# Agent attention with a squared-ReLU FFN: background blocks taken in pairs, four single banks a set, and a reordered start

## The chip, the cores and the metric

The kernel runs on one core of a Trainium2 chip. The metric is the device time of one execution in microseconds (us); a comparison uses the median of several runs. Engines are named as in the profile: PE (matmul), PEld (its weight loads), DVE (vector), ACT (scalar), POOL (GpSimd), SP (issues DMAs). [...]

## What is computed

```python
def _attn_ref(q, k, v, agents):                # B, N, C = 4, 12480, 128; 49 agents
    scale = 1.0 / np.sqrt(q.shape[-1])
    def sm(a, b):
        s = scale * (a @ b.transpose(0, 2, 1))
        s = s - s.max(-1, keepdims=True)
        e = np.exp(s)
        return e / (e.sum(-1, keepdims=True) + 1e-09)
    a2k = sm(agents, k)
    agent_v = a2k @ v
    q2a = sm(q, agents)
    return (q2a @ agent_v).astype(np.float32)

def _moe_ref(x, w_in, w_out):                  # 49920 tokens, d_ff 2048
    h = np.maximum(x @ w_in, 0.0)
    return (h * h @ w_out).astype(np.float32)
```

## The kernel before, in words

The agents' values of a batch (49 x 128) are multiplied with `w_in` into tables (`aw_hi`, and `aw_ex` for the rest of their precision). The first product of the FFN is then table times query weights: `w` (128 rows) against `aw_hi`, and the strips `x` (19 rows) against `aw_ex`. Each fp32 product of the second half is made of three rounded ones: `g_lo` x `wo_hi`, `g_hi` x `wo_lo`, `g_hi` x `wo_hi`.

**Sessions.** The main loop (lines 766 to 827) runs 211 sessions of up to 8 chunks of 128 hidden units for 480 tokens; 52 of them make a batch. The first four (EARLY) have 4 chunks, sessions 4 to 207 have 8. In session s, PE makes the `first` product (line 393) into bank set x and then y, four banks each; the sets A and B alternate. Then PE makes the `second` product (line 433) of session s-2: 24 matmuls of 480 columns (12 if that session had 4 chunks), all into bank 0 of x, after ACT has rectified it. ACT rectifies the banks (`rectified`, line 417, one instruction per entry of GROUPS, line 161) and squares the result `r` (line 421). DVE rounds `r` of the session before into `g_hi`, subtracts twice for `g_lo` (lines 808 to 823, "low part" below), and at the end of the session copies or adds bank 0 into `ob` (line 447), which frees that bank for the set that takes it next. So a bank 0 that DVE frees late holds up the `first` product of the next session, whose second set is that bank's.

**Attention beside it.** Everything else is cut into steps with a session and a phase ("P" on PE, "D" on DVE, "A1", "A3" on ACT, "L" for loads). After LEAD = 6 matmuls of `second`, phase "P" runs. There stand, for short:
- Q: query scores of a group of 960 tokens, 64 records of matmuls with 49 columns in the trace (32 in the order, since each is recorded twice), once in four sessions. DVE then makes `m`, `e`, ACT the exponential, DVE `z` (four instructions) and `pp`;
- T: one of two transpositions of `pp` per group; ACT casts the bank to `w`;
- K and V: a block of 1024 keys (scores, ACT copy `s`, DVE running maximum `mx`) or of values (DVE difference `d`, ACT exponential, matmuls, DVE `av` and `mx`) of the next batch, 13 each, also 64 records of 49 columns;
- W: one of four tables of the next batch.

`plan` (lines 729 to 739) gives the queries their sessions: scores AHEAD = 6 sessions ahead of use. `allowed` (line 741) lets the background of the next batch take one step in each even session, and in an odd one if it is behind its schedule; BEGIN and SPARE shift this schedule. So Q, K and V come in sessions of their own or together, one block each.

**The start.** `head` (lines 533 to 706) makes the agents' values of batch 0 with banks of its own, decodes the weights, which come as pairs of 32-bit words, in chunks of 512 columns (ACT, four or five DVE instructions, then `kept`: a cast on ACT and two instructions on POOL), and makes tables 0 and 1 and `aw_ex`. Tables 2 and 3 are made in sessions 0 and 1 in a spare set B. While s < 4 the sessions use set A alone, B takes those tables, the first query scores and the outputs `o` of sessions 2 and 3 (two banks, by turns). The tiles of the last weight chunk, called `s` in the trace, come from pool `sp`, which is closed with the head; the pool of `r` and `g_lo` is opened after that in the same memory.

Of the kernel before, what the change touches and what calls it, by code (L numbers as in the profile page):

```python
# [9 lines left out]
F32 = mybir.dt.float32  # L10
# [7 lines left out]
P = 128  # L18
TP = 120
NT = 8  # L20
# [8 lines left out]
AHEAD = 6  # L29
# [7 lines left out]
BEGIN = 4  # L37
SPARE = 3
# [3 lines left out]
def agent_attention_relu2(ctx: ExitStack, tc: tile.TileContext, qT, kT, v, agT, w_in, w_out, outT):  # L42
# [49 lines left out]
    ps_h = head.enter_context(tc.tile_pool(name="ps_h", bufs=3, space=PSUM))  # L92
    ps_o = head.enter_context(tc.tile_pool(name="ps_o", bufs=1, space=PSUM))
    ps_a = head.enter_context(tc.tile_pool(name="ps_a", bufs=1, space=PSUM))
# [53 lines left out]
    def kept(at, t, rest):  # L148
# [6 lines left out]
        act.copy(hi, t)  # L155
        pool.tensor_sub(t, t, hi.bitcast(F32))
        pool.tensor_add(lo, t, rest)
# [3 lines left out]
    GROUPS = ((0, 1), (1, 1), (2, 2))  # L161
# [9 lines left out]
    def bank():  # L171
        if alone[0]:
            return ps_h.tile([P, 2, 512], F32, name="h")[:, 0, :]
        return desk["at"][BLOCKS]
# [31 lines left out]
    def scores(b, i, kt):  # L206
        st = state.setdefault(b, {"s": []})
        _, rows, nt = blocks[i]
        sv = bank()[:rows, : nt * NA].rearrange("p (t a) -> p t a", a=NA)
        for t in range(nt):  # L210
            tiled(sv[:, t, :], kt[:, t * rows : (t + 1) * rows], ag[:, b, :])
        s = sp.tile([P, NT * NA], F32, name="s").rearrange("p (t a) -> p t a", a=NA)
        st["s"].append(s)
        if i == 0:
            st["mx"] = small.tile([P, NT, NA], F32, name="mx")
        s, mx = (x[:rows, :nt, :] for x in (s, st["mx"]))
        yield "A1", 0
        act.copy(s, sv)
        yield "D", 0
        if i == 0:  # L220
            dve.tensor_copy(mx, s)
        else:
            dve.tensor_max(mx, mx, s)

    def maxima(b):
        st = state[b]
        m1 = small.tile([P, NA], F32, name="m1")
        dve.reduce_max(m1, st["mx"].rearrange("p t a -> p a t"), axis=AX.X)
        yield "P", 1, True
# [7 lines left out]
        yield "P", 1, True  # L237
# [19 lines left out]
    def whole_sums(b):  # L257
# [7 lines left out]
        yield "P", 1, True  # L265
# [7 lines left out]
    def values(b, i, vt):  # L273
        st = state[b]
        _, rows, nt = blocks[i]
        yield "D", 0, True
        es = st["mx"][:rows, :nt, :]
        e = small.tile([P, NT, NA], F32, name="d", bufs=2)[:rows, :nt, :] if i else es
        less_maximum(b, i, e, spare())
        yield "A3", 0  # L280
        act.activation(e, e, AF.Exp, scale=scale)
        yield "P", 1
        pv = bank()
        for t in range(nt):
            tiled(pv[:C, :NA], vt[:rows, t, :], e[:, t, :], start=(t == 0), stop=(t == nt - 1))
        yield "D", 0
        if i == 0:
            st["av"] = small.tile([C, NA], F32, name="av")
            dve.tensor_copy(st["av"], pv[:C, :NA])
        else:  # L290
            dve.tensor_add(st["av"], st["av"], pv[:C, :NA])
            spare().tensor_add(es, es, e)

    def tables(b):
# [4 lines left out]
        for n in range(FF // 512):  # L299
            yield "P", 1, True  # L300
# [19 lines left out]
    def queries(g):  # L320
# [24 lines left out]
        for j in range(2):  # L345
            yield
            pt = query_bank(TURNED)
# [110 lines left out]
    def background(b):  # L458
        kt = load_keys(b, 0, kv, "kt")
        for i in range(NK):  # L460
            yield "P", 1, True
            nxt = load_keys(b, i + 1, kv, "kt") if i + 1 < NK else load_values(b, 0, kv, "vt")
            yield from scores(b, i, kt)
            kt = nxt
        yield from maxima(b)
        vt = kt
        for i in range(NK):
            nxt = load_values(b, i + 1, kv, "vt") if i + 1 < NK else None
            yield from values(b, i, vt)
            vt = nxt  # L470
        yield from whole_sums(b)
        yield from tables(b)

    EVENTS = 2 * NK + 3 + FF // 512
# [18 lines left out]
    even = const.tile([P, 512], F32R, name="even")  # L493
    nc.gpsimd.memset(even.bitcast(F32), 1.0)

# [5 lines left out]
    idled(ps_a, (512,) * 7 + (G,) * 4)  # L501

# [4 lines left out]
    def table(n, pieces=1):  # L507
        near = aw.tile([P, 512], F32R, name="aw_lo", bufs=3)
        pws = [bank() for _ in range(pieces)] if n < 2 else [desk["at"][4 - n]]
        w = 512 // pieces  # L510
# [10 lines left out]
    def rest_of_tables():  # L521
        near = aw.tile([P, 512], F32R, name="aw_lo", bufs=3)
        pw = ps_a.tile([P, 512], F32, name="psa")
# [9 lines left out]
    with tc.tile_pool(name="pre", bufs=PRE) as pre, tc.tile_pool(name="dec", bufs=2) as dec:  # L533
        H = P // 2
# [34 lines left out]
        def keeps(at):  # L569
            kept(at, *raws.pop(at))  # L570
# [15 lines left out]
        todo["next"] = (*next(todo["gen"]), 0)  # L586
# [106 lines left out]
        bounds(2 * FF - WIDE)  # L693
# [17 lines left out]
    sets = ctx.enter_context(tc.tile_pool(name="sets", bufs=1, space=PSUM))  # L711
# [17 lines left out]
    for g in range(1, B * NB):  # L729
        gen = queries(g) if g > 1 else ahead  # L730
        u = starts[g] - AHEAD
        if g > 1:
            plans(gen, (u - 2, "L"))
        t0, t1 = u + 3, u + 5
        if g == 1:
            u, t0, t1 = 1, 4, 5
        plans(gen, (u, "P"), (u, "D"), (u, "A3"), (u + 1, "D"), (u + 1, "A3"), (u + 2, "D"))
        for t in (t0, t1):
            plans(gen, (t, "P"), (t, "A1"), (t, "A1"))

    def allowed(s):
        if s < todo["start"]:
            return False
        if s % 2 == 0:
            return True
        return todo["done"] < (s - todo["start"] + 1) * EVENTS / (todo["end"] - todo["start"] - SPARE)

    def phase(name, s):
        for gen in plan.pop((s, name), ()):
            step(gen)  # L750
        while todo["next"]:
            (at, lead, *event), since = todo["next"][:-1], todo["next"][-1]
            if at != name or s < since + lead:
                break
            if event:
                if not allowed(s if name == "P" else s + 1):
                    break
                todo["done"] += 1
            said = step(todo["gen"])
            todo["next"] = said and (*said, s)  # L760

    made, x, early = {}, None, None
    todo["end"] = starts[NB]
    for s in range(len(sessions) + LAG):
# [3 lines left out]
        if s in starts and s // 2 and starts.index(s) % NB == 0:  # L768
            assert not todo["next"]
            b = starts.index(s) // NB  # L770
            if b + 1 < B:
                todo.update(gen=background(b + 1), done=0, start=s, end=starts[(b + 1) * NB])
                todo["next"] = (*step(todo["gen"]), s)
        phase("L", s)

        tags = "AB" if s <= len(EARLY) or (s - len(EARLY)) % 2 == 0 else "BA"
        x = Banks(tags[0])
        other = lambda: Banks(tags[1])
        if s == 0:
            early = other()  # L780
        desk["at"] = early if s < len(EARLY) else x
        o = desk["at"][s % LAG if s < len(EARLY) else 0][:, :G]
# [6 lines left out]
        if s < LAG:  # L789
            alone[0] = True  # L790
            if s:
                for _ in range(5):
                    pe.matmul(desk["at"][0][:, :P], ones, ones, start=True, stop=True)
            table(s + 2)
            alone[0] = False
# [7 lines left out]
        if m == 2:  # L803
            squared(r, 0, 2 * SET)
        elif m:
            for n in (0, 2):
                squared(r, n, 2)
        if 1 <= s <= len(sessions):
            z, n = sessions[s - 1]
            old = made.pop(s - 1)  # L810
            hi = held("g_hi", F32R, n, place(z)[2] % (2 * SET))
            los = [ffn.tile([P, SET, G], F32R, name="g_lo", bufs=3) for _ in range(n)]
            parts[z] = hi, los
            if n == 2:
                rounded(hi, old, 0, 2 * SET)
                rest(los[0], old, hi, 0, SET)
                phase("D", s)
                rest(los[1], old, hi, SET, SET)
            else:
                for i in (0, 2):  # L820
                    rounded(hi, old, i, 2)
                    rest(los[0], old, hi, i, 2)
                phase("D", s)
# [3 lines left out]
        phase("A3", s)  # L827

# [34 lines left out]
```

## Time and profile before

| | us |
|---|---|
| median of 3 runs (1887.86 to 1888.83) | 1888.68 |
| the profiled execution's own time | 1887.94 |
| its span | 1885.8 |
| PE busy | 1859.1 |
| DVE busy | 1715.7 |
| ACT busy | 1623.9 |
| POOL busy | 21.0 |

The profiled execution is 0.74 us below the median, and 2.1 us of its time lie outside the span. A timeline row gives start, length and instruction, rows of one kind in a row merged with their count; neighbouring instructions of an engine overlap at their ends, so the cost of one is read from start to start. A bracket names idle time ahead of the instruction and the engine that ended it.

### The profile page before, as it was taken

The numbers are of one execution on the slowest core, as the hardware profiler recorded it, in microseconds if no ns is written. First come the engines' busy times: TensorE is split into PE (matmuls) and PEld (weight loads), VectorE is DVE, ScalarE is ACT, GpSimd is POOL, SyncE is SP. The second block draws the span as 40 slices with busy tenths as digits, with TensorE's granted clock in tenths as the row PEclk, the third lists the DMA queues.
The fourth block names the chain that finished last, engine by engine and source line by source line (L and its number), as shares of the span: only waits on it lengthen the run. The fifth ranks groups of instructions, "written<-read, shape, count | busy, mean of one in ns | idle before, by whom it ended". The sixth has DMA issues, their size and how long they took to land.

```text
span 1885.8 us, 39996 instructions
## 1 busy us (share of the span) xinstructions
PE 1859.1 (99%) x17186; PEld 1464.5 (78%) x17186; DVE 1715.7 (91%) x1487; ACT 1623.9 (86%) x1834; POOL 21.0 (1%) x24
## 2 busy tenths in 40 slices
PE   8899999999999999999999999999999999999998
PEld 4577877877778878777778787878777877877787
DVE  7799899999899899999998899999999999999997
ACT  5688888888888888888898888888888998999996
POOL 2100000000000000000000000000000000000000
PEclk9999999999999999999999999999999999999999
DMA  9222212211122222321112221322111111111100
GB/s 374 87 90 85 82 54 77 94 61 52 54 72 78 87 61 67 95 70 59 56 42 78 94 64 33 94 73 68 52 40 43 46 39 51 40 44 45 37 27 24
DMA packets 54820, 131.47 MB, mean 70 GB/s; under 512 B 6508, under 2 KB 34828, under 8 KB 54644
## 3 DMA queue, kind: packets, MB, share of 16 engines
q1 hardware_dynamic: 54644, 128.93, 21.4%
q8 instruction: 135, 2.21, 0.5%
q14 instruction: 41, 0.34, 0.1%
HBM read 80.97 MB, written 25.56 MB: 56 GB/s over the span
## 4 chain that ended last, share of the span: by engine, by line
PE 90%; DVE 8%; ACT 1%; issue 1%; POOL 0%; DVEq 0%; ACTq 0%; POOLq 0%
PE A L63 46%; PE B L63 42%; DVE g_lo L63 3%; DVE g_hi L63 2%; DVE ob L63 1%; DVE mx L63 1%; DVE z L63 1%; DVE e L63 1%; DVE t L63 0%; PE h L63 0%; ACT r L63 0%; DVE rest L63 0%; PE o L63 0%; PE psa L63 0%; DVE d L63 0%
## 5 line engine op out<-in xcount | busy, mean ns | idle before, releaser
L63 DVE TENSOR_TENSOR g_lo<-r,g_hi 128x1920 fp32r<-128x1920 f32 (+1 forms) x422 | 894.5, 2126 | 7.5
L63 ACT ACTIVATE r<-r 128x3840 f32<-128x3840 f32 (+1 forms) x217 | 719.5, 3319 | 2.2
L63 ACT ACTIVATE r<-B 128x480 f32<-128x480 f32 (+1 forms) x618 | 393.3, 723 | 132.1 <-PE B L63 132.1
L63 ACT ACTIVATE r<-A 128x480 f32<-128x480 f32 (+1 forms) x630 | 400.8, 723 | 71.4 <-PE A L63 71.4
L63 DVE CAST g_hi<-r 128x3840 fp32r<-128x3840 f32 (+1 forms) x217 | 448.6, 2067 | 1.7 <-ACT r L63 1.7
L63 PE MATMUL A<-g_hi,wo_lo 128*128 128x480 f32 x832 | 328.4, 395 | 0.0
L63 PE MATMUL B<-g_hi,wo_lo 128*128 128x480 f32 x832 | 324.9, 390 | 1.3 <-ACT r L63 0.7
L63 PE MATMUL A<-g_hi,wo_hi 128*128 128x480 f32 x832 | 317.2, 381 | 0.0
L63 PE MATMUL B<-g_hi,wo_hi 128*128 128x480 f32 x832 | 316.6, 381 | 0.0
L63 PE MATMUL A<-w,aw_hi 128*128 128x480 f32 x840 | 230.0, 395 | 3.6 <-ACT r L63 2.0
L63 PE MATMUL B<-w,aw_hi 128*128 128x480 f32 x824 | 223.8, 393 | 0.0
L63 PE MATMUL A<-g_lo,wo_hi 128*128 128x480 f32 x832 | 215.1, 380 | 0.6 <-ACT r L63 0.6
L63 PE MATMUL B<-g_lo,wo_hi 128*128 128x480 f32 x832 | 214.9, 380 | 0.6 <-ACT r L63 0.6
L63 PEld LDWEIGHTS A<-w,aw_hi 128*128 128x128 f32 x840 | 150.0, 188 | 59.5 <-issue 34.0
L63 PEld LDWEIGHTS B<-w,aw_hi 128*128 128x128 f32 x824 | 146.7, 188 | 49.8 <-issue 30.7
L63 PEld LDWEIGHTS A<-g_hi,wo_lo 128*128 128x128 f32 x832 | 156.6, 188 | 30.2 <-issue 2.4
L63 PEld LDWEIGHTS B<-g_hi,wo_lo 128*128 128x128 f32 x832 | 156.5, 188 | 27.4 <-DVE g_hi L63 1.3
L63 PEld LDWEIGHTS A<-g_hi,wo_hi 128*128 128x128 f32 x832 | 156.6, 188 | 25.6 <-issue 2.2
L63 PEld LDWEIGHTS A<-g_lo,wo_hi 128*128 128x128 f32 x832 | 156.2, 188 | 25.9 <-ACT r L63 0.9
L63 PEld LDWEIGHTS B<-g_lo,wo_hi 128*128 128x128 f32 x832 | 156.2, 188 | 25.8 <-ACT r L63 0.9
L63 PEld LDWEIGHTS B<-g_hi,wo_hi 128*128 128x128 f32 x832 | 156.3, 188 | 23.4 <-issue 0.7
L63 DVE COPY ob<-A 128x480 f32<-128x480 f32 x103 | 67.7, 657 | 61.6 <-PE A L63 58.3
(169 smaller groups left out, 1280.6 us busy)
## 6 DMA issues: line engine op xcount, KB each, us to landing
qt<-in_qT SPq DMA_DIRECT2D x52, 480.0 KB
out_T<-ob SPq DMA_DIRECT2D x104, 240.0 KB
kt<-in_kT SPq DMA_DIRECT2D x36, 512.0 KB
vt<-in_v SPq DMA_DIRECT2D x36, 512.0 KB
x<-w SPq DMA_DIRECT2D x416, 35.6 KB
ahead<-in_kT SPq DMA_DIRECT2D x12, 512.0 KB
ahead<-in_v SPq DMA_DIRECT2D x12, 512.0 KB
w<-w SPq DMA_DIRECT2D x104, 56.2 KB
```

Source lines behind the costliest of these rows:

```text
L63: ins = issue(*args, **kw)
```

## The change

1. Background blocks: `room(s)` gives two blocks to the sessions that have query scores, and one to an even session if the schedule is behind; no block stands in another session. `scores` and `values` take a group of one or two, the second in the bank TURNED. The loads are issued by `more()` in phase "L".
2. GROUPS has four single banks, so a set is rectified by four instructions instead of three.
3. Queries: AHEAD is 8, the transpositions stand one session apart, the second in bank ASKED; FIRSTS gives the first three groups their sessions. BEGIN is 6, SPARE 9.
4. Head: its banks are closed before the tables, which go into set B (table 0 in banks 0 and 1, `aw_ex` in 2, table 1 in 0, tables 2 and 3 in banks 2 and 3). The last weight chunk is bounded, decoded and kept behind the tables, and kept by DVE alone.
5. Start: a session with 4 chunks makes its low part itself, not the session after; sessions 0 and 1 square ahead of their table; sessions 4 and 5 square and round in halves and end with eight small matmuls on `ones`.

```diff
-AHEAD = 6
+AHEAD = 8
-BEGIN = 4
-SPARE = 3
+BEGIN = 6
+SPARE = 9
...
-    GROUPS = ((0, 1), (1, 1), (2, 2))
+    GROUPS = ((0, 1), (1, 1), (2, 1), (3, 1))
...
-    def scores(b, i, kt):
...
+    def scores(b, group):
+        st = state.setdefault(b, {"s": []})
+        outs = []
+        for (i, kt), slot in zip(group, (BLOCKS, TURNED)):
+            _, rows, nt = blocks[i]
+            sv = bank(slot)[:rows, : nt * NA].rearrange("p (t a) -> p t a", a=NA)
+            for t in range(nt):
+                tiled(sv[:, t, :], kt[:, t * rows : (t + 1) * rows], ag[:, b, :])
+            outs.append(sv)
...
-            pt = query_bank(TURNED)
+            pt = query_bank((TURNED, ASKED)[j])
...
-        bounds(2 * FF - WIDE)
         warm(ps_a, 3)
         pa = bank()
         pe.matmul(pa[:, :P], avs, spread, start=True, stop=True)
         warm(ps_a, 2)
         turn["avT"] = small.tile([C, P], F32, name="av0")
         dve.tensor_copy(turn["avT"], pa[:, :P])
+        banks.close()
+        sets = ctx.enter_context(tc.tile_pool(name="sets", bufs=1, space=PSUM))
+        early = desk["at"] = Banks("B")
+        table(0, (0, 1))
+        rest_of_tables()
+        table(1, (0,))
+        bounds(2 * FF - WIDE)
         makes(2 * FF - WIDE)
-
-        table(0, 2)
-        rest_of_tables()
-        keeps(2 * FF - WIDE)
-        table(1)
+        keeps(2 * FF - WIDE, dve)
...
+    def room(s):
         if s < todo["start"]:
-            return False
-        if s % 2 == 0:
-            return True
...
+            return 0
+        if s % 4 == starts[1] % 4:
+            return 2
+        late = todo["done"] < (s - todo["start"] + 1) * 2 * NK / (todo["end"] - todo["start"] - SPARE)
+        return int(late and s % 2 == 0)
...
+    def idle(n):
+        for _ in range(n):
+            pe.matmul(desk["at"][BLOCKS][:, :P], ones, ones, start=True, stop=True)
+
+    def low_parts(z, s=None):
...
         if s < LAG:
+            if s:
+                idle(5)
+                phase("P", s)
+            for n in (0, 2):
+                squared(r, n, 2)
             alone[0] = True
...
-            table(s + 2)
+            table(s + 2, (s + 2,))
...
+        if s - 1 in made:
+            low_parts(s - 1, s)
+        if m == 1:
+            low_parts(s)
         run(work)
         if s >= LAG:
             copied_out(*sessions[s - LAG], o)
         phase("A3", s)
+        if len(EARLY) <= s < BEGIN:
+            idle(8)
```

**The end of the head on DVE.** `s` is the last weight chunk, `aw_hi` and `aw_ex` are tables. Before:

```order
L63 SCALAR_TENSOR_TENSOR s<-vt,s 128x512
L63 TENSOR_SCALAR s<-s 128x512
L63 SCALAR_TENSOR_TENSOR s<-vt,s 128x512
L63 SCALAR_TENSOR_TENSOR aw_hi<-h,signs,aw_lo 128x256 x2
L63 TENSOR_TENSOR aw_ex<-psa,aw_lo 128x512
L63 SCALAR_TENSOR_TENSOR aw_hi<-h,signs,aw_lo 128x512
L63 SCALAR_TENSOR_TENSOR aw_hi<-B_741,signs,aw_lo 128x512
```

Now:

```order
L68 SCALAR_TENSOR_TENSOR aw_hi<-B_686,signs,aw_lo 128x512
L68 TENSOR_SCALAR s<-s 128x512 x2
L68 SCALAR_TENSOR_TENSOR s<-vt,s 128x512
L68 TENSOR_SCALAR s<-s 128x512
L68 SCALAR_TENSOR_TENSOR s<-vt,s 128x512
L68 CAST wo_hi<-s 128x512
L68 TENSOR_TENSOR s<-s,wo_hi 128x512
L68 TENSOR_TENSOR wo_lo<-s 128x512
L68 SCALAR_TENSOR_TENSOR aw_hi<-B_688,signs,aw_lo 128x512
```

The decode stood ahead of the tables and now stands behind table 1, and the three instructions that keep the chunk follow it on DVE. The first rectification on ACT (`r_750<-A0`), which takes memory of these tiles, has among the engines it waits for DVE and POOL before, and the same now.

**Sessions 2 and 3 on DVE**, from the `z` of the first group to the second output. Before:

```order
L63 TENSOR_TENSOR e<-e,z 120x392
L63 COPY ob<-B_739 128x480
L63 CAST g_hi<-r 128x960
L63 TENSOR_TENSOR g_lo<-r,g_hi 128x960
L63 CAST g_hi<-r 128x960
L63 TENSOR_TENSOR g_lo<-r,g_hi 128x960
L63 TENSOR_TENSOR pp<-e,pp 120x8x49
L63 TENSOR_TENSOR ob<-B_740,ob 128x480
```

Now:

```order
L68 TENSOR_TENSOR e<-e,z 120x392
L68 CAST g_hi<-r 128x960
L68 TENSOR_TENSOR g_lo<-r,g_hi 128x960
L68 CAST g_hi<-r 128x960
L68 TENSOR_TENSOR g_lo<-r,g_hi 128x960
L68 COPY ob<-B_686 128x480
L68 TENSOR_TENSOR pp<-e,pp 120x8x49
L68 CAST g_hi<-r 128x960
L68 TENSOR_TENSOR g_lo<-r,g_hi 128x960
L68 CAST g_hi<-r 128x960
L68 TENSOR_TENSOR g_lo<-r,g_hi 128x960
L68 TENSOR_TENSOR ob<-B_687,ob 128x480
```

One whole low part, four instructions, that of session 3, now stands ahead of the second `ob`.

**A block in the value phase, on PE** (T and V in one session). Before:

```order
L63 MATMUL B_8243<-identr,pp 98x120 x4
L63 MATMUL B_8242<-d,vt 32x49 x32
L63 MATMUL B_8241<-g_hi,wo_lo 128x480
L63 MATMUL B_8241<-g_hi,wo_hi 128x480
L63 MATMUL B_8241<-g_hi,wo_lo 128x480
```

Now, in a session with query scores:

```order
L68 MATMUL A_3635<-ag,qt 24x49
L68 MATMUL A_3634<-d,vt 32x49 x32
L68 MATMUL A_3636<-d,vt 32x49 x32
L68 MATMUL A_3633<-g_hi,wo_lo 128x480
L68 MATMUL A_3633<-g_hi,wo_hi 128x480
```

Two blocks follow the scores directly, each in its own bank. **On DVE the session ahead of such a pair** now holds the group's `pp` and two `d`:

```order
L68 CAST g_hi<-r 128x3840
L68 TENSOR_TENSOR g_lo<-r,g_hi 128x1920
L68 TENSOR_TENSOR pp<-e,pp 120x8x49
L68 TENSOR_TENSOR d<-s,mb 128x392 x2
L68 TENSOR_TENSOR g_lo<-r,g_hi 128x1920
L68 TENSOR_TENSOR ob<-B_4464,ob 128x480
```

Before, the fullest session of a cycle in that phase held the group's `z` and one block:

```order
L63 CAST g_hi<-r 128x3840
L63 TENSOR_TENSOR g_lo<-r,g_hi 128x1920
L63 TENSOR_REDUCE z<-e 120x8
L63 TENSOR_SCALAR z<-z 120x8
L63 RECIPROCAL z<-z 120x8
L63 TENSOR_TENSOR e<-e,z 120x392
L63 TENSOR_TENSOR av<-av,B_3932 128x49
L63 TENSOR_TENSOR mx<-mx,d 128x392
L63 TENSOR_TENSOR d<-s,mb 128x392
L63 TENSOR_TENSOR g_lo<-r,g_hi 128x1920
L63 TENSOR_TENSOR ob<-B_3931,ob 128x480
```

The `d` of a pair moved into a session that has no Q, K, V or T on PE.

## Rows read from the trace of the kernel before

**Rows 1.** PE timeline, starts of sessions 52 to 55 (start, us, instruction)

```profile
509.15 1.03 PE L63 MATMUL A<-w,aw_hi 128*128 128x480 f32 x4
...
517.98 1.02 PE L63 MATMUL B<-w,aw_hi 128*128 128x480 f32 x4
...
526.15 1.03 PE L63 MATMUL A<-w,aw_hi 128*128 128x480 f32 x4
...
533.97 1.03 PE L63 MATMUL B<-w,aw_hi 128*128 128x480 f32 x4
```

**Rows 2.** PE timeline, Q and K together in session 8

```profile
124.00 0.90 PE L63 MATMUL A<-ag,qt 128*32 128x49 f32 x64
124.71 0.87 PE L63 MATMUL A<-ag,kt 128*32 128x49 f32 x64
```

**Rows 3.** DVE timeline, sessions 6 and 7

```profile
108.29 0.56 DVE L63 TENSOR_TENSOR pp<-e,pp 120x392 fp32r<-120x392 f32 x1
108.77 0.56 DVE L63 TENSOR_TENSOR mx<-mx,s 128x392 f32<-128x392 f32 x1
...
112.03 0.66 DVE L63 COPY ob<-A 128x480 f32<-128x480 f32 x1 [0.63 <-PE A L63]
...
114.79 4.23 DVE L63 TENSOR_TENSOR g_lo<-r,g_hi 128x1920 fp32r<-128x1920 f32 x2
```

**Rows 4.** PE timeline, session 38, with one V, and the start of 39

```profile
385.74 1.03 PE L63 MATMUL A<-w,aw_hi 128*128 128x480 f32 x4
...
387.35 0.49 PE L63 MATMUL B<-x,aw_ex 19*128 19x480 f32 x4 [0.17 <-DVE ob L63]
...
395.03 1.03 PE L63 MATMUL B<-w,aw_hi 128*128 128x480 f32 x4
```

**Rows 5.** Groups by form, ACT, 105 to 1860 us (busy us, mean ns | idle before, releaser)

```profile
L63 ACT ACTIVATE r<-B 128x480 f32<-128x480 f32 x406 | 212.1, 584 | 131.2 <-PE B L63 131.2
...
L63 ACT ACTIVATE r<-B 128x960 f32<-128x960 f32 x203 | 203.3, 1001 | 0.0
```

**Rows 6.** DVE timeline, head: an earlier chunk's decode, and table 1

```profile
33.95 0.88 DVE L63 TENSOR_SCALAR t<-t 128x512 f32<-128x512 f32 x2
...
36.05 0.69 DVE L63 SCALAR_TENSOR_TENSOR rest<-raw,rest 128x512 f32<-128x512 uint32 x1
...
60.06 0.75 DVE L63 SCALAR_TENSOR_TENSOR aw_hi<-h,signs,aw_lo 128x512 fp32r<-128x512 f32 x1 [0.44 <-ACT aw_lo L63]
```

**Rows 7.** ACT timeline, first rectifications of sessions 0 and 1

```profile
62.55 1.89 ACT L63 ACTIVATE r<-A 128x480 f32<-128x480 f32 x3 [2.52 <-PE A L63]
...
66.90 1.88 ACT L63 ACTIVATE r<-A 128x480 f32<-128x480 f32 x3
```

**Rows 8.** DVE timeline, sessions 2 and 3

```profile
78.18 0.55 DVE L63 TENSOR_REDUCE z<-e 120x8 f32<-120x392 f32 x1
...
79.69 0.65 DVE L63 COPY ob<-B 128x480 f32<-128x480 f32 x1
...
84.26 0.65 DVE L63 TENSOR_TENSOR ob<-B,ob 128x480 f32<-128x480 f32 x1
```

**Rows 9.** PE timeline, sessions 1 and 4 to 8

```profile
66.28 1.38 PE L63 MATMUL B<-ones 128*128 128x128 f32 x10
...
84.96 0.48 PE L63 MATMUL B<-x,aw_ex 19*128 19x480 f32 x3 [1.46 <-DVE ob L63]
...
86.55 0.60 PE L63 MATMUL A<-g_hi,wo_lo 128*128 128x480 f32 x1
...
92.56 1.03 PE L63 MATMUL B<-w,aw_hi 128*128 128x480 f32 x4
...
100.11 1.03 PE L63 MATMUL A<-w,aw_hi 128*128 128x480 f32 x4
...
104.17 0.49 PE L63 MATMUL B<-x,aw_ex 19*128 19x480 f32 x4 [1.80 <-DVE ob L63]
...
120.03 1.03 PE L63 MATMUL A<-w,aw_hi 128*128 128x480 f32 x4
```

More of the change, by code (lines that the diff above doesn't have):

```diff
@@ L146, in decoded, with kept @@
         return t.bitcast(F32), rest
-    def kept(at, t, rest):
+    def kept(at, t, rest, *only):
         n = t.shape[1]
@@ L271, in whole_sums, with values @@
         dve.reciprocal(rl, rl)
-    def values(b, i, vt):
+    def values(b, group):
         st = state[b]
[L275 to L279, printed above, removed]
-        yield "A3", 0
[L281 to L285, printed above, removed]
-        yield "D", 0
[L287 to L292, printed above, removed]
+        es, outs = [], []
+        for i, _ in group:
+            _, rows, nt = blocks[i]
+            e = small.tile([P, NT, NA], F32, name="d", bufs=2) if i else st["mx"]
+            es.append(e[:rows, :nt, :])
+            less_maximum(b, i, es[-1], spare())
+        yield "A3", 0
+        for e in es:
+            act.activation(e, e, AF.Exp, scale=scale)
+        yield "P", 1, "told"
+        for (i, vt), e, slot in zip(group, es, (BLOCKS, TURNED)):
+            _, rows, nt = blocks[i]
+            pv = bank(slot)
+            for t in range(nt):
+                tiled(pv[:C, :NA], vt[:rows, t, :], e[:, t, :], start=(t == 0), stop=(t == nt - 1))
+            outs.append(pv)
+        yield "D", 0
+        for (i, _), pv in zip(group, outs):
+            if i == 0:
+                st["av"] = small.tile([C, NA], F32, name="av")
+                dve.tensor_copy(st["av"], pv[:C, :NA])
+            else:
+                dve.tensor_add(st["av"], st["av"], pv[:C, :NA])
+        for (i, _), e in zip(group, es):
+            if i:
+                _, rows, nt = blocks[i]
+                all_e = st["mx"][:rows, :nt, :]
+                spare().tensor_add(all_e, all_e, e)
     def tables(b):
@@ L751, in phase @@
         while todo["next"]:
-            (at, lead, *event), since = todo["next"][:-1], todo["next"][-1]
-            if at != name or s < since + lead:
+            (at, lead, *gate), since = todo["next"]
+            if at != name or s < since + lead or gate and not allowed(name, s, *gate):
                 break
[L755 to L758, printed above, removed]
             said = step(todo["gen"])
-            todo["next"] = said and (*said, s)
-    made, x, early = {}, None, None
+            todo["next"] = said and (said, s)
+    def idle(n):
+        for _ in range(n):
+            pe.matmul(desk["at"][BLOCKS][:, :P], ones, ones, start=True, stop=True)
+    def low_parts(z, s=None):
+        k, n = sessions[z]
+        r = made.pop(z)
+        hi = held("g_hi", F32R, n, place(k)[2] % (2 * SET))
+        los = [ffn.tile([P, SET, G], F32R, name="g_lo", bufs=3) for _ in range(n)]
+        parts[k] = hi, los
+        if n == 1:
+            for i in (0, 2):
+                rounded(hi, r, i, 2)
+                rest(los[0], r, hi, i, 2)
+            return
+        apart = z < BEGIN
+        rounded(hi, r, 0, SET if apart else 2 * SET)
+        rest(los[0], r, hi, 0, SET)
+        if apart:
+            rounded(hi, r, SET, SET)
+        phase("D", s)
+        rest(los[1], r, hi, SET, SET)
+    made, x = {}, None
     todo["end"] = starts[NB]
@@ L803, in agent_attention_relu2 @@
         if m == 2:
-            squared(r, 0, 2 * SET)
-        elif m:
+            for n in (0, SET) if s < BEGIN else (0,):
+                squared(r, n, SET if s < BEGIN else 2 * SET)
+        elif m and s >= LAG:
             for n in (0, 2):
                 squared(r, n, 2)
[L808 to L823, printed above, removed]
+        if s - 1 not in made:
+            phase("D", s)
+        if s - 1 in made:
+            low_parts(s - 1, s)
+        if m == 1:
+            low_parts(s)
         run(work)
@@ L827, in agent_attention_relu2 @@
         phase("A3", s)
+        if len(EARLY) <= s < BEGIN:
+            idle(8)
+    assert not plan and not todo["next"]
 _NAMES = ["qT", "kT", "v", "agT", "w_in", "w_out"]
```

153 lines of the change are left out of this document (87 added, 66 removed), and 3 rows, old and new, of the table FIRSTS.

## The prediction

> **What bounds the kernel now.** The table of the profile comes first: PE is busy for 1859.1 of 1885.8 us, DVE for 1715.7, ACT for 1623.9. So time is gained where PE has less to do, or waits less. I then read PE's timeline by sessions. A plain session takes 7.82 us (526.15 to 533.97), one with T 8.17, one with Q 8.83 [rows 1]. The order says which sessions hold which steps; a session's length is the plain one plus a price for each step, wherever DVE keeps up. So the steady part, sessions 8 to 208, can be priced by counting.
>
> Where DVE doesn't keep up, the place is bank 0. DVE frees it with `ob` at the end of its list, and the next session's `first` needs it. DVE's fixed list is 2.76 us for `ob` and `g_hi` (112.03 to 114.79) and 4.23 for both `g_lo`, 6.99 in all; `pp` or a block instruction adds 0.48 [rows 3], `z` with its three companions 1.51 (78.18 to 79.69) [rows 8]. Session 37 has T, `z` and one `d`: 8.98 on DVE against 8.17 on PE, 0.81 too much. Session 38 then takes 9.29 (385.74 to 395.03), where a V alone should take 8.83, and shows the wait for `ob` [rows 4]. So of an excess of 0.81, 0.46 arrive on PE; some 0.35 are absorbed. I use this rule below.
>
> ACT waits for PE at each set: 131.2 us ahead of one form alone [rows 5]. It is not the bound on the average.
>
> The start is different: until session 7 PE waits on DVE again and again (84.96: 1.46 us, 104.17: 1.80 us) [rows 9]. There the sum goes by the chain, not by counts.
>
> **Pairs of blocks (gain).** A block's 64 records take 0.71 us when they follow Q directly (124.00 to 124.71) [rows 2]. Q alone adds 1.01 to a session [rows 1], so entering and leaving such a stretch costs 0.30. Q and K of that row lie in different banks, and K pays no second entry. The same is assumed for the second block of a pair. By the order, 97 of sessions 8 to 208 hold a stretch of Q, K or V before and 70 now; the number of blocks in them is the same, and W, the maxima and the sums are as many as before. So 27 entries go: 27 x 0.30 = **-8.1 us**. One transposition more falls into these sessions: +0.35 [rows 1].
>
> **DVE beside them (small loss).** Two `d` and `pp` now stand in the plain session ahead of a pair in the value phase: 6.99 + 3 x 0.48 = 8.43 against 7.82, 0.61 too much, by the rule 0.26 each, ten times: 2.6. The pair's own session has 6.99 + m, e, two `av`, two `mx`, about 9.3, under its 10.25 (7.82 + 0.30 + 3 x 0.71). The sessions with `z` and a block, where it waited before, lose some of their waits. Going through all 201 sessions with the rule gives 6.3 us of such waits before and 6.8 now: **+0.5**. The steady part together: **-7.25**. The new loads, `kt` and `vt` in phase "L", come two blocks ahead; SP's queue in front of the `w` and `x` copies gets no longer, so I set them at nothing, and a late `x` would show as a wait for a DMA.
>
> **Single banks (hidden).** Each session gets two rectifications more. The row of three (480, 480, 960 columns) took 1.89 us [rows 7]; four of 584 ns that overlap in the same way come to 1.92, so 0.03 to 0.05 each. By durations it is 2 x 584 - 1001 = 167 ns [rows 5]. ACT waits for PE in most sessions, which hides either, except in the sessions that hold T and `pp`: there the sum by the low price is some 8.05 against PE's 8.17. I take the low price, since it comes from instructions in a row, and nothing on the path. [...]
>
> **The start (loss).** Four edits meet here.
> - ACT's first rectification started at 62.55 [rows 7]. Its tile reuses memory of the last weight chunk, so it has to wait until this chunk has been kept. The order shows the chunk's decode and keep on DVE behind table 1, which ended at 60.06 + 0.75 [rows 6]. The decode is 33.95 to 36.74 for an earlier chunk, 2.8 us [rows 6]; the keep is three instructions of 512 columns that the trace doesn't show on DVE, between 0.47 and 0.69 each by their neighbours; I take 1.9. That gives 65.5. Since the decode no longer stands ahead of the tables, they may come up to 0.6 earlier. I take 65.2, 2.65 later than before.
> - One round of rectifying, squaring and a table on ACT is 66.90 - 62.55 = 4.35 [rows 7]. Two of them end at 73.9; then DVE makes the last table (0.7), `m` and `e` (1.1) and a low part (3.5: 84.26 - 79.69, less `ob` 0.57 and `pp` 0.48 [rows 8]). So the `z` that stood at 78.18 comes at 79.2. The reordered squares gain nothing, since DVE has the low part of session 0 in the meantime.
> - From `z` to the second `ob` before: 6.1 us [rows 8]. Now the low part of session 3 stands ahead of that `ob`: 3.5 more. It starts at 88.8 instead of 84.26, or up to 0.6 less. PE's `x` product into that bank, at 84.96 before, comes at about 89.2: **+4.2**.
> - From there to session 5 it was 7.6 us (84.96 to 92.56). K leaves (-0.7); eight matmuls on `ones` come: five, recorded as ten, took 1.38 with the overlap, about 0.25 each [rows 9], so +2.0. That is 8.9. Session 5 took 7.55; K (1.0) and a wait for ACT leave and 2.0 come, so 7.55 again. Sessions 6 and 7 took 19.92 (100.11 to 120.03) with the wait of 1.80 in them. Now they hold two K alone (7.82 + 0.30 + 1.42 = 9.54) and Q (8.83), and DVE's low part of session 4 is made in halves and ahead of time: no wait. Session 8 then starts at 89.2 + 8.9 + 7.55 + 18.37 = 124.0 instead of 120.03: **+4.0**.
>
> Bounds of that +4.0. After the wait at 84.96 six matmuls show 0.60 us where the rest show 0.38 (86.55) [rows 9]; PE was at the lower clock there, which cost about 1.7 us in all. I assume that a longer wait brings the same again. Without it, +2.3; with the lower clock over most of sessions 4 and 5, twice as much is lost, +6.
>
> **The sum.** -7.25 + 4.0 = -3.25 on the profiled execution's 1887.94, which is 1884.7. The median lies 0.74 above it, so 1885.4. The tail, the last three sessions, isn't changed.
>
> **Rivals.**
> 1. The start costs less: full clock after the wait in session 4, or DVE's idle time before 70 us takes up the decode entirely. Then +1.5 to +2.3, and the time is 1882.9 to 1883.7, with the waits in the value phase gone 1881. For it: DVE stands still for much of 61 to 69 us. Against it: ACT can't start before the chunk is kept, and DVE's list to the second `ob` is longer in any case.
> 2. Slower than before: ACT becomes the bound where T and `pp` meet. The point is an extra rectification of about 0.06 us; if it costs the 0.167 of the durations, such a session needs 8.3 on ACT against 8.17, about 0.16 too late, in some 50 sessions: +8, 1893.4. For it: the margin there is only 0.12. Against it: the row of three shows 1.89, where durations add to 2.17, and ACT has over 3 us spare in a cycle of four sessions.
> 3. The second block pays an entry of its own, in another bank: the 8.1 shrink to nothing, 1893 or, where half of it stays, 1889. Against it: [rows 2].
> 4. The start costs more, +6 to +8, by the lower clock or by a second wait in session 6: 1887.4 to 1889.4. For it: PE waits 4 us at 85 to 89 where it waited 1.46.
>
> **How the numbers follow.** The forecast, 1883.7 to 1887.4, has 0.50; rival 1 has 0.24; rival 4 0.12; rival 2 0.07; rival 3 0.07. About 0.2% (3.8 us) can be told from no change, so faster means under 1884.9 and slower over 1892.5. Faster takes rival 1 and two fifths of the forecast, 0.44; slower takes rival 2 and a third of rival 3, 0.09; the same 0.47. The range goes from 1881.0 to 1890.0, which leaves out rival 2, most of rival 3 and the far ends of rivals 1 and 4, some 0.2.
>
> **What would show it.** Steps right: sessions with Q and two blocks of about 10.25, T 8.17, plain 7.82, a second block 0.71 behind the first; ACT's first rectification at 65 with its wait ended by DVE; PE's wait in session 4 ended by `ob` near 89; session 8 near 124. Wrong: a gap between the two blocks' records, ACT named ahead of PE in sessions with T, or a first rectification before 63, which would take away most of the loss at the start. Waits for `ob` at the start of the value phase's pair sessions should be about 0.3; over 1 would make DVE the bound there.

## The result: slower by 1.1%, and where the time went

The changed kernel took 1909.85 us (median of 4 runs, 1905.81 to 1913.58) against 1888.72 before: a ratio of 1.0112, 95% interval 1.0092 to 1.0133. The forecast was 1885.4, in a range of 1881.0 to 1890.0. The profiled execution took 1909.94 against 1887.94, 22.0 more. Its start of sessions splits the 22.0: session 8 begins at 125.68 instead of 120.03, which is 5.65; sessions 8 to 208 take 1758.3 instead of 1741.8, which is 16.5; the tail takes 0.1 less.

PE's waits of the changed kernel (engine, line and what it waited for: us in total, times, longest) have a line that was nearly empty before (0.7 us, once):

```profile
PE A L68 <- issue: 15.5, 12, 2.1
PE h L68 <- DMA ahead<-in_kT: 5.9, 11, 1.5
PE A L68 <- ACT r L68: 5.2, 2, 4.5
PE B L68 <- DVE ob L68: 4.9, 2, 4.1
```

"issue" is a wait for nothing that the profile shows. PE's timeline puts these waits inside the stretch of Q and two blocks, and nowhere else. Session 10, then session 14 (start, length, work; in brackets the idle time ahead of it and what ended it):

```profile
146.05 0.90 PE L68 MATMUL A<-ag,qt 128*32 128x49 f32 x64
146.77 1.58 PE L68 MATMUL A<-ag,kt 128*32 128x49 f32 x128
...
152.32 1.03 PE L68 MATMUL B<-w,aw_hi 128*128 128x480 f32 x4
```
```profile
177.50 1.03 PE L68 MATMUL A<-w,aw_hi 128*128 128x480 f32 x4
...
181.48 0.90 PE L68 MATMUL A<-ag,qt 128*32 128x49 f32 x64
182.20 1.51 PE L68 MATMUL A<-ag,kt 128*32 128x49 f32 x121
185.77 0.29 PE L68 MATMUL A<-ag,kt 128*32 128x49 f32 x7 [2.07 <-issue]
...
187.05 0.60 PE L68 MATMUL A<-g_hi,wo_lo 128*128 128x480 f32 x1
...
191.57 0.60 PE L68 MATMUL B<-w,aw_hi 128*128 128x480 f32 x2
```

Session 10 (142.07 to 152.32) takes the forecast 10.25 us. Session 14 takes 14.06: after 121 of the 128 records of its blocks PE stands still for 2.07 us. Behind that the granted clock is 0.50 from 186.90 to 190.20, and a matmul takes 0.60 us, where 0.38 is usual. Stretches of session 14 (start:end, length, busy times, granted clock, DMA):

```profile
181.48:185.99 4.51, 2.44 (x193) 2.24 (x192) 2.84 (x4) 1.80 (x4) 0.00 (x0) 1.00 0.50 132
185.99:191.57 5.58, 5.58 (x26) 4.72 (x19) 2.64 (x2) 4.21 (x3) 0.00 (x0) 0.69 0.52 175
```

With 0.69 granted, the second stretch loses about 5.58 x 0.31 = 1.7 us. 2.1 and 1.7 are the 3.8 by which the session is too long. Session 90 is like it (0.50 granted from 869.60 to 872.90). The other stops brought no such drop (1.00 granted from 191 to 869 us and from 873.5 to 1900); behind that of session 66, of 1.88 us from record to record, all of the clock was granted:

```profile
652.10:657.70 5.60, 5.60 (x42) 4.57 (x45) 3.68 (x4) 4.22 (x3) 0.00 (x0) 1.00 0.58 190
```

All 24 sessions with Q and two whole blocks together take 25.5 us over 10.25 each, between none and 3.8 apiece. Added up from record to record, some 19.0 of these are gaps inside the stretches, in 18 of the sessions; 3.4 are the lower granted clock in sessions 14 and 90; 2.4 are lost at the start of ten of these sessions (0.24 each), where the forecast has 2.6 for the wait for `ob`. The other sessions from 8 to 208 gain 9.0, where the forecast has 9.85 (its 7.25, and the 2.6 that it puts at the pairs). So the count of entries was right; the pair's own price was not.

The start went nearly as forecast (the changed kernel's timeline of ACT, then of PE):

```profile
66.16 1.96 ACT L68 ACTIVATE r<-A 128x480 f32<-128x480 f32 x4 [5.51 <-DVE wo_lo L68]
```
```profile
91.27 0.77 PE L68 MATMUL B<-x,aw_ex 19*128 19x480 f32 x3 [4.09 <-DVE ob L68]
```

ACT's first rectification, at 62.55 in [rows 7], waits for the last weight chunk on DVE and starts at 66.16 (forecast 65.2). PE's `x` product, at 84.96 in [rows 9], waits for the second `ob` until 91.27 (forecast 89.2).

### The profile page after: what moved, and what is told of

It reads as the page before. It is cut to its first block, busy times and chain, and to the rows that moved or that the text cites. A ratio compares the mean times of both kernels' runs of the same rounds, so it can differ in the third digit from the quotient of the medians.

```text
span 1908.0 us, 40527 instructions
## 1 busy us (share of the span) xinstructions
PE 1864.2 (98%) x17218; PEld 1475.1 (77%) x17218; DVE 1723.6 (90%) x1492; ACT 1650.6 (87%) x2251; POOL 18.1 (1%) x22
## 3 DMA queue, kind: packets, MB, share of 16 engines
q8 instruction: 135, 2.21, 0.5%
## 4 chain that ended last, share of the span: by engine, by line
PE 92%; DVE 5%; issue 1%; DMA 0%; ACT 0%; SPq 0%; DVEq 0%; ACTq 0%
PE A L68 48%; PE B L68 44%; DVE g_lo L68 2%; DVE g_hi L68 1%; DVE mx L68 1%; DVE ob L68 0%; DMA ahead<-in_kT 0%; DVE t L68 0%; PE h L68 0%; PE o L68 0%; DVE e L68 0%; DVE rest L68 0%; DVE z L68 0%; DVE s L68 0%; SPq L68 0%
## 5 line engine op out<-in xcount | busy, mean ns | idle before, releaser
L68 ACT ACTIVATE r<-r 128x3840 f32<-128x3840 f32 (+2 forms) x219 | 721.1, 3298 | 2.6
L68 ACT ACTIVATE r<-B 128x480 f32<-128x480 f32 x824 | 407.1, 599 | 124.5 <-PE B L68 123.4
L68 ACT ACTIVATE r<-A 128x480 f32<-128x480 f32 x840 | 414.9, 599 | 67.7 <-PE A L68 62.0
L68 DVE CAST g_hi<-r 128x3840 fp32r<-128x3840 f32 (+2 forms) x219 | 449.6, 2053 | 0.8 <-ACT r L68 0.3
L68 DVE TENSOR_TENSOR ob<-B,ob 128x480 f32<-128x480 f32 x105 | 68.9, 656 | 64.1 <-PE B L68 63.6
```

Of the source, the lines that this page charges most:

```text
L68: ins = issue(*args, **kw)
```

## The experiments

Two theories of the "issue" waits stood at the outset: A, PE's supply of instructions runs dry inside a long stretch of short matmuls; B, the loads of two blocks, issued together, disturb it.

### One block at a time: single

```diff
-        if s % 4 == starts[1] % 4:
-            return 2
-        return int(late and s % 2 == 0)
+        return int(late or s % 2 == 0)
```

(The loads are issued without the step "L" of the next session.)

> The changed kernel with one block in each even session, and in an odd one if the schedule is behind; never two. 98 of sessions 8 to 208 hold a stretch of Q, K or V instead of 70. Theory A (PE runs out of instructions inside the stretch of 192 short records, stands still up to 2.1 us, and runs at the lower clock behind it): no session shows an idle PE with 'issue' over 0.5 us, the 25.5 us that the pair sessions take over 10.25 each are gone, 28 x 0.30 = 8.4 us of entries come: 1891 to 1895. Theory B (the loads of two blocks issued together disturb PE): the same, since the loads are apart too. Theory C (the loss lies elsewhere, in the single banks or on DVE): over 1900.

1890.42 us, ratio 1.0009 (0.9999 to 1.0018). One "issue" wait of 0.3 is left. Sessions 8 to 208 take 1739.4, 2.4 under the kernel before, while session 8 starts at 126.02. So the pairs are the loss of the steady part, and C falls; the late start is what keeps this version from being faster. A and B aren't told apart yet.

### The pair split: split

```diff
         phase("P", s)
+        for _ in range(12):
+            next(work, None)
+        phase("P2", s)
```

(The second block of `scores` and `values` waits for phase "P2".)

> The changed kernel, with 12 matmuls of the second product between the two blocks of a pair. Loads, DVE and ACT work as in the changed kernel. Theory A: no 'issue' wait over 0.4 us; 24 to 27 more entries of 0.30 are 7 to 8 us, the 25.5 go: 1891 to 1893. Theory B (the loads): the waits stay, somewhere in the session, and the entries come on top: about 1917.

1940.23 us, ratio 1.0275 (1.0258 to 1.0292). The "issue" waits are gone (0.8 us left), with the loads as they were: B falls. The total was far off the expected 1891 to 1893, since another wait came. The timeline of PE's session 11, and of DVE at the end of session 10:

```profile
156.76 0.49 PE L68 MATMUL A<-x,aw_ex 19*128 19x480 f32 x4 [1.04 <-DVE ob L68]
```
```profile
153.50 0.57 DVE L68 TENSOR_TENSOR mx<-mx,s 128x392 f32<-128x392 f32 x1 [2.54 <-ACT s L68]
153.98 2.15 DVE L68 TENSOR_TENSOR g_lo<-r,g_hi 128x1920 fp32r<-128x1920 f32 x1
156.05 0.65 DVE L68 COPY ob<-A 128x480 f32<-128x480 f32 x1
```

DVE's `mx` of the late block stands ahead of its second `g_lo` and of `ob`; it waits 2.5 us, and the next session waits for `ob`. The 24 sessions behind a pair take 36.7 us too much.

### The same work at another place in the program: shift

```diff
-        idled(ps_a, (512,) * 7 + (G,) * 4)
+        idled(ps_a, (512,) * 7 + (G,) * 4 + (32,) * 32)
```

> The changed kernel with 32 very short matmuls more at its start, where PE waits for the first keys: nothing in the sessions changes, but each instruction stands 64 places later in PE's program. Theory A: the point in the stretch at which PE stops depends on the place in the program, so it moves 32 records forward: session 14 from record 185 to 153, 38 from 174 to 142, 66 from 176 to 144, 90 from 166 to 134; 18, 70, 82, 110 and 122 show none; the size goes with the record as in the changed kernel (about 0.2 at 130, 1.1 at 143, 1.7 at 156, 2.2 at 185). Sessions that showed none may show one now. Theory B: the same sessions, the same records, the same sizes.

1914.51 us, ratio 1.0136 (1.0120 to 1.0151). The 32 matmuls weren't free: PE had no such gap, and session 8 starts 6.8 us later; sessions 8 to 208 take 1757.9, as in the changed kernel (1758.3). The waits moved as A says. For the sessions that tell most: the record of the stretch at which PE stops, and its longest gap between records in us, in the changed kernel and here; last, the place of that stop in PE's program, counted in instructions from the listed order (a matmul with rounded operands is two, an fp32 one four), modulo 256:

```
session   changed kernel   shift          place mod 256 (changed, shift)
14        185  2.27        153  1.96      241  241
22        165  1.40        133  0.59      233  233
38        174  1.67        142  1.14      219  219
66        176  1.88        144  0.82      195  195
78        164  1.59        132  0.52      187  187
90        166  1.92        134  0.46      175  175
118       168  1.80        136  1.28      151  151
130       156  1.67        124  0.50      143  143
18, 70    143, 134         none
34, 62    none             184  2.35, 186  2.21
86, 114   none             176  2.25, 178  1.93
```

Every stop that is in both moved by exactly 32 records, and new ones came in sessions that had none or nearly none (also in 138; that of 142 went). The place slides by some 0.86 a session, since the order leaves out the 219 semaphore instructions that the changed kernel's trace has on PE. Counted with these, all stops of over 0.4 us in the changed kernel, here and in pairs_only below lie at 37 to 44 modulo 256. PE's program has 34,542 listed instructions, and the page of the changed kernel has this line of DMA transfers (packets, MB, share):

```profile
q8 instruction: 135, 2.21, 0.5%
```

2.21 MB in 135 are 16.4 KB each, and 34,542 / 135 is 256. With the places, which agree modulo 256, I read it so: PE's instructions came in transfers of 256, and PE stopped where it had reached the end of one before it could use the next. The trace has the time of each transfer, and the two meet. In session 14 a transfer begins at 183.01 and lands at 184.30; the last record ahead of the stop starts at 183.50, the next one at 185.77, 1.47 us after the landing. All stops of over 0.4 us, with the last transfer ahead of their end (us):

```
run          stops   gap            transfer took   goes on after its landing by
changed      11      0.43 to 2.27   0.88 to 1.31    1.27 to 1.55
shift        13      0.46 to 2.35   0.92 to 1.44    1.19 to 1.50
pairs_only   15      0.54 to 2.21   0.88 to 1.34    1.31 to 1.56
```

Transfers come once in some 14 us (135 in 1908), so such an agreement isn't chance; what fills the time from the landing to the next record isn't shown. Nor were they slowed by the loads: the 135 of the changed kernel took 0.88 to 1.44 us, with a wait behind them or not. A stretch of 192 records has 384 instructions, as each has its weight load (193 and 192 in the trace of session 14), and ran in 2.1 us where it didn't stop; of the 72 such stretches in these three runs 48 show a gap of 0.09 us or more. None of the 39 stops comes before record 123: an end that lay earlier in the stretch brought no stop of over 0.4 us in these runs.

### The last weight chunk as before: keep, keep_single

```diff
+        bounds(2 * FF - WIDE)
         warm(ps_a, 3)
...
+        makes(2 * FF - WIDE)
         table(0, (0, 1))
         rest_of_tables()
+        keeps(2 * FF - WIDE)
         table(1, (0,))
-        bounds(2 * FF - WIDE)
-        makes(2 * FF - WIDE)
-        keeps(2 * FF - WIDE, dve)
```

> The changed kernel, with the last weight chunk bounded and decoded ahead of the tables and kept by ACT and GpSimd, as before. If ACT's first rectification waits for the chunk, as the trace of the changed kernel names it (66.16, waiting for wo_lo on DVE), it starts at 62.5 to 63.5 now, the second ob of DVE ends some 3 us earlier, and session 8 starts at 122 to 123.5 instead of 125.7; the total falls by 2 to 4 us, within which the waits of the pair sessions also vary. Rival: the first products or tables are what is late, then 65 to 66 and no change.

1910.04 us (1904.28 to 1913.60), ratio 1.0112: in the total nothing can be read, as the pairs' waits differ by some us from run to run. The trace shows the step (keep: ACT's timeline, then PE's):

```profile
61.59 1.96 ACT L68 ACTIVATE r<-A 128x480 f32<-128x480 f32 x4 [2.08 <-POOL wo_lo L68]
```
```profile
85.72 0.77 PE L68 MATMUL B<-x,aw_ex 19*128 19x480 f32 x3 [4.09 <-DVE ob L68]
```

The rectification comes 4.6 us earlier, the `x` product 5.5, session 8 at 120.72, 5.0 earlier. Some 1.8 of these 5 us lie ahead of the tables and need not come from the edit: the product with `avs` starts at 53.90 here and at 55.73 in the changed kernel, 55.08 in single. From 25 to 53 us the granted clock was 1.00 here and 0.88 in the changed kernel. The same edit on single shows it in the total:

> Blocks one by one as in single, and the last weight chunk decoded ahead of the tables and kept by ACT and GpSimd as in keep. Without the waits of the pair sessions the start can be read in the total. Theory (ACT's first rectification waits for the chunk on DVE): rectification at 61.5 to 62.5, session 8 at 121 to 122 instead of 126.0 in single, 1885.5 to 1887, which is 3.5 to 5 us under single. Rival (the wait moves on to another engine and the start is given back by session 8): 1889 to 1891.

1886.50 us, ratio 0.9989 (0.9979 to 0.9998), 3.9 under single. The chunk on DVE behind the tables cost 3.9 us.

### The low parts, the idle matmuls, the banks: keep_low_single, low_no_idle, low_groups

```diff
+            phase("D", s)
...
-        if s - 1 not in made:
-            phase("D", s)
-        if s - 1 in made:
+        if 1 <= s <= len(sessions):
             low_parts(s - 1, s)
-        if m == 1:
-            low_parts(s)
```

> As keep_single, and the low part of a session with 4 chunks is made in the session after, as before, so that the low part of session 3 stands behind the second ob on DVE. Theory (the low part of 3.5 us ahead of that ob holds PE's x product in session 4): that product comes at about 82 instead of 85.7, PE's wait of 4.1 us shrinks to under 1, session 8 starts 3 to 3.5 us earlier, 1882 to 1884. Rival (what is late next, the low part of 3 for session 5, gives it back): no better than keep_single by more than 1 us.

1885.86 us, ratio 0.9986 (0.9977 to 0.9996), 0.6 under keep_single, which is within the spread. Session 4 waits 1.6 us instead of 4.1, but session 2 now waits for the low part of session 0, which comes behind the last table (PE's timeline):

```profile
72.45 0.48 PE L68 MATMUL B<-g_hi,wo_lo 128*128 128x480 f32 x1 [1.54 <-DVE g_hi L68]
```

Session 8 starts at 122.50 (122.34 in keep_single; the profiled execution here was the slowest of ten, 1888.30, so the totals say more). My expectation fell; the wait moved to another session.

Without the eight matmuls on `ones`:

```diff
-        if len(EARLY) <= s < BEGIN:
-            idle(8)
```

> As keep_low_single, without the eight matmuls on ones at the end of sessions 4 and 5. If they only fill time in which PE would wait for ACT and DVE in any case, the same as keep_low_single within 1 us; if they are on the path, 2 x 1.95 = 3.9 us less; if they hold the clock up, up to 2 us more.

1884.94 us, ratio 0.9983 (0.9974 to 0.9993): 0.9 less, not told apart. In the trace sessions 4 and 5 get shorter and session 6 longer (12.71 instead of 8.93).

Three rectifications a set, on keep_low_single:

```diff
-    GROUPS = ((0, 1), (1, 1), (2, 1), (3, 1))
+    GROUPS = ((0, 1), (1, 1), (2, 2))
```

> As keep_low_single, with three rectifications a set again (480, 480, 960 columns) instead of four. If ACT is hidden behind PE throughout, the same within 1 us; if the eight instructions a session held PE up in sessions with T, less by up to 8 us; if single banks hand the bank on earlier, more.

1884.61 us, ratio 0.9981 (0.9972 to 0.9991): 1.2 less, hardly more than the spread. Nothing says that eight rectifications held PE up, though ACT was busy for 25.6 us less here (1626.9 instead of 1652.5), 62 ns for each of 416 instructions. In this trace session 4 ran at the full clock (9.64 us at 1.00 granted, 14.16 at 0.76 in keep_low_single); whether the banks or chance did that stays open.

### The pairs alone: pairs_only

The pairs of the changed kernel, with their loads, on low_groups:

```diff
+                    yield "L", 1
...
+        if s % 4 == starts[1] % 4:
+            return 2
-        return int(late or s % 2 == 0)
+        return int(late and s % 2 == 0)
```

> low_groups with the pairs of the changed kernel back: two blocks in each session with query scores, 70 stretches instead of 98; the start and the banks as in low_groups. It prices the pairs alone. Theory A (PE runs out of instructions in a stretch of 192 short records at a fixed place of each 256 instructions): -28 x 0.30 and some 20 to 30 us for the waits and the lower clock behind them, 1897 to 1907; sessions 14, 22, 38, 66, 78, 90, 118 and 142 wait over 1 us, as in the changed kernel. Rival (the loss of the changed kernel comes from its start or its banks): 1876 to 1885.

1917.63 us, ratio 1.0151 (1.0135 to 1.0166), 33.0 over low_groups and 10 over what was expected. All eight sessions named wait over 1 us (1.60 to 2.21 between two records). PE waits 22.5 us for "issue", and the pair sessions take 30.5 over 10.25 each. Besides, each session behind a pair takes about 0.3 too long (6.9 in 24). Banks 2 and 3 are one tile here, the scores of Q lie in the one and the second block in the other. DVE's `m`, which reads the scores, starts only when ACT has copied the second block; so DVE's list ends later, and PE waits for `ob` at the start of the next session (sessions 10 and 11 of pairs_only: ACT and DVE, then PE and its weight load):

```profile
142.28 0.49 ACT L68 COPY s<-A 128x392 f32<-128x392 f32 x1 [0.21 <-PE A L68]
142.80 0.57 DVE L68 TENSOR_REDUCE m<-A 120x8 f32<-120x392 f32 x1 [1.18 <-ACT s L68]
147.03 0.65 DVE L68 COPY ob<-A 128x480 f32<-128x480 f32 x1
```
```profile
147.12 0.49 PE L68 MATMUL B<-x,aw_ex 19*128 19x480 f32 x4
147.73 0.49 PE L68 MATMUL A<-x,aw_ex 19*128 19x480 f32 x4
147.73 0.19 PEld L68 LDWEIGHTS A<-x,aw_ex 19*128 19x128 f32 x4 [0.41 <-DVE ob L68]
```

The first of PE's rows takes 0.32 us to the next elsewhere, here 0.61. Over the whole run `m` waits 34.3 us for ACT's `s`, in 12 sessions, and 25.7 for PE, in 14; in the changed kernel it waits once, at the start, and the sessions behind a pair lose 0.4 in 24. By 6.9 and 0.4 the single banks are worth some 6 us with pairs (an estimate; no run changes the banks alone beside pairs).

### Pairs in a shorter stretch, or at a harmless place: pairs_aside, pairs_aware, pairs_aside_later

On pairs_only, the pairs go from the sessions with Q to those with T:

```diff
-        if s % 4 == starts[1] % 4:
+        if s % 4 == (starts[1] + 2) % 4:
             return 2
```

> low_groups with pairs in every fourth session, but in the one with the second transposition, not in the one with query scores; where the schedule is behind, one block beside the scores. No stretch has more than 128 short records, 256 instructions; 80 stretches of Q, K or V instead of 98. Theory A: a stretch that is no longer than the 256 instructions that PE has in hand waits little, none over 1 us (as the 26 stretches of Q and K of the kernel before, of which one waited 0.9): -18 x 0.30 = -5.4, 1878 to 1881. Rival (a second block on its own brings the wait, whatever the length, or DVE's list with z and two blocks, 9.7 us against PE's 9.9, becomes late): 1885 to 1900.

1882.96 us, ratio 0.9972 (0.9961 to 0.9984). In session 8 the second block of a pair and the first transposition of the second group share a bank, so that group of 960 tokens is computed from other numbers; the amount of work is the same. PE's session 12, with T and two blocks:

```profile
158.43 0.48 PE L68 MATMUL A<-identr,pp 120*98 120x120 f32 x4
158.84 1.59 PE L68 MATMUL A<-ag,kt 128*32 128x49 f32 x128
```

None of the 26 such sessions waits for "issue" over 0.1 us, and they sum to 0.5 us under their price (7.82 + 0.35 + 0.30 + 2 x 0.71 = 9.89; this one took 9.86). So two blocks in two banks went without a second entry here, and 128 records in a row without a wait of over 0.1 us. That PE has 256 instructions in hand, as the expectation puts it, isn't shown; the traces show transfers of that size. Of the expected -5.4 only 1.7 came, 0.6 of it in sessions 8 to 208 of the two traces: the sums of each batch and the maxima stand in plain sessions now and wait for `ob` (3.2 us in three sessions).

On low_groups, a pair beside Q stands only where by the count no wait is due:

```diff
+        if s % 4 == starts[1] % 4:
+            stop = (253 - 0.86 * s - begins_at(s)) / 2 % 128
+            return 2 if 76 <= stop <= 124 else 1
...
-        return int(late or s % 2 == 0)
+        return int(late)
```

(`begins_at` counts PE's instructions up to the stretch of session s.)

> low_groups with two blocks beside the scores only in sessions 14, 22, 26, 34, 66, 110 and 118, where by the count of PE's instructions (the fixed place read from the changed kernel's traces) no wait is due; one block elsewhere; 90 stretches instead of 98. Theory A: none of the seven waits over 0.5 us, -8 x 0.30 = -2.4, 1881.5 to 1883. Rival (the wait goes with the transfers of the moment, not with the place in the program): about half of the seven wait 0.5 to 2 us, 1885 to 1892.

1885.39 us, ratio 0.9981 (0.9972 to 0.9991). Of the seven sessions, which were chosen by the count alone (in 22 the second block has 12 records only, the other six pairs are whole), two show a gap, of 0.26 and 0.16 us. That bears A out where it could have failed. The total lies in the rival's range all the same. The gain of 2.4 didn't come: 2.6 us were lost behind the pairs, where `m` waits 8.6 us for ACT's `s` and 2.3 for PE in seven sessions, as in pairs_only.

Last, pairs_aside without the pair in session 8:

```diff
-        if s % 4 == (starts[1] + 2) % 4:
+        if s % 4 == (starts[1] + 2) % 4 and s > 8:
```

> As pairs_aside, with the pairs from session 12 on; session 8, where the early transposition of the second group needs the bank of a pair's second block, takes one block at most. The work and the 80 stretches are otherwise the same. If the length of the stretch is what counts, 1882 to 1884, 5 to 7 us under the kernel before, as pairs_aside; no wait of PE for its instructions over 0.3 us in sessions 9 to 208. Rival (pairs_aside was fast by chance of its place in the program): 1885 to 1889.

1884.11 us, ratio 0.9979 (0.9970 to 0.9988). Here every group has its own numbers again, and this version is faster than both kernels, 4.5 us under the one before; one wait of 0.6 for "issue" is left, in session 122 in a stretch of 128 records, where at most 0.3 was expected. So a stretch of 128 isn't safe in itself; this was its one wait, where pairs_only has 16. The total isn't told apart from low_groups (1884.61): the blocks in pairs gave little beyond the start and the schedule.

## Why the prediction was wrong

- **The step that failed** is "The same is assumed for the second block of a pair", and with it 10.25 us for a pair's session. That no second entry is paid was right (session 10, and pairs_aside). That the length of the stretch changes nothing was not: 24 sessions took 25.5 us more. Some 19.0 of them are gaps in the stretch, 17.6 of that in the 11 stops of over 0.4 us, which ended 1.27 to 1.55 us after a transfer of instructions had landed; 3.4 are the lower granted clock (0.50) behind two of these gaps, and 2.4 the loss at the start of the session that was forecast for `ob`. [rows 2] shows two blocks' worth of records, 128, and the sum took its price on to 192.
- The trace of before held the hint. In its one long session 136 (10.52 instead of 9.53), Q and V stop one record before the end:

```profile
1253.92 0.89 PE L63 MATMUL A<-d,vt 128*32 128x49 f32 x63
1255.54 0.23 PE L63 MATMUL A<-d,vt 128*32 128x49 f32 x1 [0.73 <-issue]
```

I had no cause for this wait and left it out of the sum. 26 stretches had 256 instructions, and one fell so that a transfer's end and its own end met: a transfer landed at 1254.09, PE went on at 1255.54, and the stop's place is 44 modulo 256. A stretch of 384, by transfers of 256, always has such an end inside it. None of the rivals named it, so the range had no place for it.
- **The steady rest**: forecast -9.85 outside the pairs' sessions, measured -9.0. Right but for 0.85.
- **DVE in the value phase**: forecast 0.26 of wait ahead of each pair; sessions 34 and 86, free of an "issue" wait, took 10.49, 0.24 over. Right.
- **Single banks**: hidden, as forecast (low_groups against keep_low_single); rival 2 (ACT late) didn't happen. What they are good for I missed: the bank of the second block (pairs_only).
- **The start**: forecast +4.0, measured +5.65. Every wait named came, by `wo_lo` and by `ob`; 1.2 of the difference arose ahead of the tables (the `avs` product at 55.73 instead of 54.53, with 0.88 granted from 25 to 53 us instead of 0.94), where nothing shows that an edit caused it. From 85 to 100 us the granted clock was 0.77 instead of 0.89, 1.8 us more lost; the sum had taken the loss of before (0.50 granted from 86.20 to 89.40 there, about 1.7 us) to come again, with twice as much as its upper bound. By keep_single the chunk's place was worth 3.9. That the low part of session 3 ahead of `ob` is what costs is not borne out: taken back, it gave 0.6, as another wait came.

## What to carry to other kernels

Count instructions, not only time: here runs of 192 short records (384 instructions in 2.1 us) stopped for up to 2.35 us, beside the transfers of 256 that brought PE's instructions, and so the price of one more block wasn't the price of its records. Before lengthening such a run, look in the trace for "issue" waits in the ones that are there, even a single one, ask what is special about its place, and set the times of the instruction transfers beside it. And where a step is moved behind another on an idle engine, look at who reuses its memory: here the next phase's first buffer waited for a weight chunk that it didn't need.

## What the runs showed of the hardware

By the counts above, PE's instructions came in transfers of 256 (16.4 KB, 0.88 to 1.44 us each in the changed kernel). In all 39 stops of over 0.4 us inside runs of short matmuls (changed kernel, shift, pairs_only) PE went on 1.19 to 1.56 us after such a transfer had landed, and the stops lay at 37 to 44 modulo 256 in PE's program. Runs of 192 short records (384 instructions) showed a gap in two of three cases, up to 2.35 us between two records. Runs of 128 (256 instructions) waited once in 26 in the kernel before (0.73 us), once in pairs_aside_later (0.6 us) and in single (0.3 us), and never over 0.1 us in 26 of pairs_aside.

PE's granted clock fell behind two of the ten stops of over 1 us in the changed kernel (0.50 from 186.90 to 190.20 and from 869.60 to 872.90; 0.69 over the 5.58 us behind the 2.07 us wait of session 14, where 480 columns took 0.60 us instead of 0.38). That cost 1.7 us each time. Behind a stop of 1.88 us in session 66 it stayed at 1.00. What decides it isn't shown.
